# Pooled values by way of a buffer in DRAM, transfers on GpSimd's queue, and another order, in a kernel of pooled attention and mixture of depths

## The chip, the cores and the metric

One core of a Trainium2 chip runs the whole program. Its engines work side by side, each through a queue of its own: PE (matmuls, with the weight load PEld), DVE (vector), ACT (activations), POOL (GpSimd) and SP, which here only issues transfers. All transfers, whoever issues them, run on the core's 16 DMA engines. PSUM, which PE writes, has eight banks; SBUF holds the tiles. The metric is the device time of one execution in microseconds.

## What is computed

The reference, cut. q, k and v are float32 of (8 batches, 8 heads, 576 tokens, 64); the weights are 512 x 1024 and 1024 x 512; capacity is 128.

```python
k_p = k.reshape(B, H, Sp, 8, D).mean(axis=3)        # Sp = 72 pooled keys and values
v_p = v.reshape(B, H, Sp, 8, D).mean(axis=3)
attn = softmax(q @ k_p^T / sqrt(D));  x = attn @ v_p # then (B, S, H*D)
scores = x @ w_gate
for b in range(B):
    top = indices of the 128 highest scores[b]
    ye = relu(x[b, top] @ w1) @ w2
    out[b] = x[b];  out[b, top] += sigmoid(scores[b, top]) * ye
```

## The kernel before

The work is written as some 770 steps. Each step has an engine (or a choice of two), what it reads and writes, and a name. A class Plan can order them by costs; here it is given three tables instead: ORDER is the sequence in which the steps are emitted, and so the order in each engine's queue; HOMES says which PSUM banks each PE job gets; TURNS says which engine of its choices a step takes. Engines wait for one another by semaphores that follow from the tiles read and written.

Per batch there is a **front** and a **dense** part. The front:
- loads the keys (KR, one buffer), the queries (QR, two) and the values (VR, two); a partition of KR and QR holds 36 consecutive tokens of a head, 16 partitions a head;
- pools keys (L498, L499: sums of fours), transposes them in blocks of 32 on DVE (kh, L507), adds the two halves (kt, L512) and sets the eight left-over pooled keys apart (kl, L517);
- transposes the queries on DVE (qt, L526), makes scores on PE (L544, L553) and their exponentials on ACT (em, el);
- pools the values (pool_v): they are loaded with a pooled row of eight tokens in one partition, 64 partitions for each parity of the heads, in eight transfers a batch, and added in three steps, 4 + 4, 2 + 2, 1 + 1 (L571, L575, L576). The sums go to VS, with a column of eights and, after a product with the gate weights (L580, L584), a column of gate scores; VL spreads the left-over rows (L588);
- attends in five chunks of tokens on PE (L605, L609), divides (L632, L633) and stores the rows of x to the output (five transfers);
- ranks: score rows are spread over partitions by PE (L670), copied (sr, L393 or L395), compared on DVE (cmp, L682), made one-hot (oh, L688), and PE **picks** (L694) the chosen tokens' numbers and scores, five columns in one PSUM bank, which DVE reads in two instructions, tk (L698) and gv (L711); POOL makes indices (ix, L702) and gathers 128 rows of x back from the output (xr, L703).

The dense part transposes the gathered rows (L724), multiplies by w1 in eight groups (L733) with relu (ht), by w2 in eight groups (L747), adds (y, L752) and scatters the rows to the output (L756). PE also runs sixteen groups of matmuls on the identity (L775) that nobody reads.

PSUM is three tiles for Plan: pG with four banks, pA and pJ with two each. Transfers of SP and ACT take turns on eight semaphores, so that a transfer waits for the one eight before it. ACT's queue holds transfers between its activations, and SP's holds only transfers; both run strictly in order.

Of the kernel before, what the change touches and what calls it, by code (L numbers as in the profile page):

```python
# [16 lines left out]
def kernel(  # L17
# [58 lines left out]
"""  # L76
HOMES = """
# [3 lines left out]
"""  # L81
TURNS = """
# [165 lines left out]
def direct_path(ctx, tc, q, k, v, moe_w_gate, moe_w1, moe_w2, moe_capacity, out, flag):  # L248
# [46 lines left out]

    KR = sb("kr", [128, TG, D])
    QR = [[sb(f"qr{i}{h}", [128, hi - lo, D]) for h, (lo, hi) in enumerate(HALF)] for i in range(2)]
    VR = sb("vr", [128, NP + 1, POOLW * D], n=2)
    KS = sb("ks", [128, R, D])
    KH = sb("kh", [128, 2, 2 * G, R])  # L300
    KT = sb("kt", [128, 2, 2, SP], n=2)
# [263 lines left out]
    def pool_v(b):  # L565
# [13 lines left out]
        def gate(e):  # L579
            engine(e).tensor_tensor(out=x[:, :, 2], in0=VS[i][:, :, 0:D], in1=WG, op=OP.mult)  # L580
# [603 lines left out]
```

## Time and profile before

| | us |
|---|---|
| runs: median of 2 (lowest, highest) | 309.18 (308.87, 309.48) |
| the profiled execution | 306.87 |
| its span in the trace | 305.0 |
| PE, DVE, POOL, ACT busy in the span | 239.0, 163.6, 126.6, 48.1 |

The rows quoted below come from the profiled execution. Its granted clock of TensorE was 0.908 of full speed on average. A busy PE is one with a matmul under way, whose ends the profile models. "Idle before" names what ended an engine's waiting, as the semaphores let it be inferred.

### The profile page before, as it was taken

How to read it: one execution, taken by the hardware profiler on the slowest of the kernel's cores; microseconds unless marked ns; L12 is line 12 of the kernel's file. 1: busy time of each engine (PE TensorE's matmuls, PEld its weight loads, DVE VectorE, ACT ScalarE, POOL GpSimd, SP SyncE). 2: the span in 40 equal slices, each digit the busy share in tenths (PEclk: the TensorE clock that was granted, in tenths of full speed). 3: DMA queues.
4: the chain of work that ended last, by engine and by line, in shares of the span. 5: the costliest groups of instructions: out<-in, count | busy, mean ns of one | idle time of the engine just before them, and what ended most of it. 6: DMA issues, size and time to landing. Idle time of an engine off the chain costs nothing. (4 is left out here: it accounts for less than half of the span.)

```text
span 305.0 us, 7299 instructions
## 1 busy us (share of the span) xinstructions
PE 239.0 (78%) x3090; PEld 165.3 (54%) x3090; DVE 163.6 (54%) x361; ACT 48.1 (16%) x134; POOL 126.6 (42%) x158
## 2 busy tenths in 40 slices
PE   7395769487597959899859997988667568999980
PEld 7263547156484534688626456768337345688530
DVE  3459592693789746597589697645144320200320
ACT  0021204031214312213210121420002100000000
POOL 3435941665677295789388453100110203100111
PEclk9867979779999986999977999999975969999996
DMA  7989939799977899688863602205120012000001
GB/s 257 201 263 163 376 91 243 222 348 227 368 255 234 198 334 290 164 269 209 269 228 118 177 24 73 90 13 167 49 78 25 0 34 71 0 34 2 34 35 45
DMA packets 18361, 47.87 MB, mean 157 GB/s; under 512 B 2320, under 2 KB 2320, under 8 KB 17424
## 3 DMA queue, kind: packets, MB, share of 16 engines
q1 hardware_dynamic: 9992, 25.37, 28.7%
q10 hardware_dynamic: 7048, 17.76, 20.2%
q0 software_dynamic: 1280, 4.20, 4.2%
q8 instruction: 26, 0.43, 0.6%
q14 instruction: 15, 0.12, 0.2%
HBM read 35.78 MB, written 11.53 MB: 155 GB/s over the span
## 5 line engine op out<-in xcount | busy, mean ns | idle before, releaser
L682 DVE SCALAR_TENSOR_TENSOR cmp<-sr,sc,lat 128x576 bf16<-128x576 f32 (+1 forms) x40 | 39.8, 995 | 10.5 <-ACT sr L393 9.7
L544 PE MATMUL pG<-qt,kt 32*64 32x320 f32 (+1 forms) x512 | 22.8, 468 | 14.7 <-DVE qt L526 5.3
L733 PEld LDWEIGHTS pJ<-xg,w 128*128 128x128 f32 x224 | 26.9, 193 | 5.5 <-issue 3.4
L733 PE MATMUL pJ<-xg,w 128*128 128x128 f32 x224 | 28.4, 278 | 1.6 <-DVE tk L698 1.6
L756 POOL DMA_INDIRECT out_dram<-y,ix x8 | 8.2, 1022 | 47.7 <-DVE y L752 41.7
L747 PE MATMUL pA<-w,ht 128*128 128x512 f32 x48 | 26.8, 677 | 1.0 <-ACT ht L740 1.0
L526 DVE STREAM_TRANSPOSE qt<-qr 128x1280 f32<-128x1280 f32 (+1 forms) x16 | 21.7, 1364 | 9.7 <-DMA qr<-in_q_dram 9.7
L702 POOL TENSOR_SCALAR ix<-tk 128x1 int32<-128x1 f32 x8 | 3.0, 370 | 55.9 <-DVE aux L656 22.6
L747 PE MATMUL pJ<-w,ht 128*128 128x512 f32 x48 | 23.4, 607 | 2.0 <-ACT ht L740 2.0
L544 PEld LDWEIGHTS pG<-qt,kt 32*64 32x64 f32 x512 | 10.3, 142 | 23.2 <-POOL kt L512 6.2
L733 PEld LDWEIGHTS pA<-xg,w 128*128 128x128 f32 x160 | 19.8, 195 | 5.2 <-issue 3.6
L498 POOL TENSOR_TENSOR kr<-kr 128x640 f32<-128x640 f32 (+1 forms) x14 | 20.4, 1458 | 5.1 <-DMA kr<-in_k_dram 5.0
L733 PE MATMUL pA<-xg,w 128*128 128x128 f32 x160 | 20.9, 280 | 1.1 <-ACT xg L393 0.7
L558 ACT ACTIVATE em<-pG 128x1280 f32<-128x1280 f32 (+1 forms) x16 | 18.1, 1128 | 22.4 <-PE pG L553 12.1
L571 POOL TENSOR_TENSOR vr<-vr 128x1280 f32<-128x1280 f32 x6 | 17.4, 2894 | 8.4 <-DMA vr<-in_v_dram 8.1
L733 PEld LDWEIGHTS pG<-xg,w 128*128 128x128 f32 x128 | 18.4, 224 | 3.9 <-issue 1.9
L733 PE MATMUL pG<-xg,w 128*128 128x128 f32 x128 | 19.3, 311 | 0.8 <-ACT xg L393 0.7
L747 PE MATMUL pG<-w,ht 128*128 128x512 f32 x32 | 16.9, 649 | 0.9 <-ACT ht L740 0.7
L688 DVE TENSOR_SCALAR oh<-slots,rk 128x128 bf16<-128x128 f32 x40 | 16.3, 469 | 0.0
L575 POOL TENSOR_TENSOR vr<-vr 128x640 f32<-128x640 f32 x8 | 12.4, 1547 | 8.3 <-DVE every L487 5.2
L605 PE MATMUL pG<-vs,em 64*64 64x66 f32 x480 | 11.9, 222 | 4.8 <-DVE xs L633 2.3
L633 DVE TENSOR_TENSOR xs<-pG,rz 128x512 f32<-128x512 f32 (+1 forms) x17 | 11.7, 690 | 6.5 <-PE pG L609 4.8
(152 smaller groups left out, 390.8 us busy)
## 6 DMA issues: line engine op xcount, KB each, us to landing
kr<-in_k_dram SPq DMA_DIRECT2D x4, 1152.0 KB
out_dram<-xs SPq DMA_DIRECT2D x17, 256.0 KB
out_dram<-xs ACTq DMA_DIRECT2D x15, 256.0 KB
kr<-in_k_dram ACTq DMA_DIRECT2D x3, 1152.0 KB
vr<-in_v_dram SPq DMA_DIRECT2D x9, 384.0 KB
w<-in_moe_w_dram SPq DMA_DIRECT2D x3, 1024.0 KB
vr<-in_v_dram ACTq DMA_DIRECT2D x7, 384.0 KB
qr<-in_q_dram ACTq DMA_DIRECT2D x4, 640.0 KB
```

The costliest lines, as they stand in the source:

```text
L498: e.tensor_tensor(out=x[:, a:z, 0:2], in0=x[:, a:z, 0:2], in1=x[:, a:z, 2:4], op=OP.add)
L526: nc.vector.transpose(out=QT[b % 2][h].rearrange("p j t c -> p t j c"), in_=QR[b % 2][h].rearrange("p t (j e) -> p t j e", j=2))
L544: nc.tensor.matmul(pG[64 * s : 64 * s + 64, r, 0:n], KT[i][rows, j, s, 0:NK], tokens(j, s, rows, 0, hi - lo), start=(j == 0), stop=(j == 1))
L558: nc.scalar.activation(EM[h][i], pG[:, :, 0:n], AF.Exp, scale=exp_scale)
L571: engine(e).tensor_tensor(out=x[:, :, 0:4], in0=x[:, :, 0:4], in1=x[:, :, 4:8], op=OP.add)
L575: engine(e).tensor_tensor(out=x[:, :, 0:2], in0=x[:, :, 0:2], in1=x[:, :, 2:4], op=OP.add)
L605: nc.tensor.matmul(acc[64 * z : 64 * z + 64, s, E * m : E * m + E], EM[h][i][64 * s : 64 * s + 64, m, m0 + 64 * z : m0 + 64 * z + 64], VS[ ...
L633: nc.vector.tensor_tensor(out=XS[i][c][rows].rearrange("p (m s d) -> p s m d", s=2, d=D), in0=o[:, :, :, 0:D], in1=rz.rearrange("p (s m on ...
L682: nc.vector.scalar_tensor_tensor(cmp[0:n], SR[0:n], SC[i][0:n, c : c + 1], LAT[0:n, LAST - OFF[c] : LAST - OFF[c] + S], op0=OP.subtract, o ...
L688: nc.vector.tensor_scalar(OH[:, c, :], slots, RK[:, b, c], None, op0=OP.is_equal)
L733: nc.tensor.matmul(single(ju)[:, cap * f : cap * f + cap], w1[g][:, d, 128 * f : 128 * f + 128], XG[i][:, d, :], start=(d == 0), stop=(d = ...
L747: nc.tensor.matmul(single(jd)[0:cap, :], HT[i][f // 4][:, f % 4, :], w2[f // 4][:, f % 4, :], start=(f == 0), stop=(f == FB - 1))
```

## The change

The values are loaded like the keys, 36 consecutive tokens of a head in a partition, in one transfer a batch. Two steps add them to sums of four tokens (VH, nine half sums a partition), which a transfer stores to a buffer in DRAM, half_sums. Six transfers read them back in the order of the pooled keys, the two half sums of one pooled value beside each other (V2, two buffers), and a third step (L589 in the changed kernel) adds these to VS. The product with the gate weights gets a tile of its own (VM). Transfers may also be issued by POOL; the new TURNS puts thirteen there: the keys of batches 1, 2 and 4, the values of 5, seven stores (six of x, one of half sums) and two read-backs. ORDER and HOMES are new throughout. Up to the first lines of the tables the diff is whole:

```diff
--- before.py
+++ after.py
@@ -46,54 +46,54 @@
 ORDER = """
-    9 2 4 767 3 5 761 760 23 10 757 768 754 22 25 24 26 12 18 17 19 16 20 34 21 11 8 6 27 28 35 36 766 14 39 13 40
...
+    2 4 774 16 0 6 770 772 762 3 5 768 765 14 10 18 9 17 766 11 776 19 20 22 21 763 771 32 33 23 24 767 761 87 34
...
@@ -295,7 +295,10 @@
 
     KR = sb("kr", [128, TG, D])
     QR = [[sb(f"qr{i}{h}", [128, hi - lo, D]) for h, (lo, hi) in enumerate(HALF)] for i in range(2)]
-    VR = sb("vr", [128, NP + 1, POOLW * D], n=2)
+    VR = sb("vr", [128, TG, D], n=2)
+    VH = sb("vh", [128, R, D])
+    V2 = sb("v2", [128, NP + 1, 2, D], n=2)
+    VM = sb("vm", [128, NP + 1, D])
     KS = sb("ks", [128, R, D])
     KH = sb("kh", [128, 2, 2 * G, R])
     KT = sb("kt", [128, 2, 2, SP], n=2)
@@ -363,6 +366,7 @@
         return pG[:, x] if x < 4 else (pA, pJ)[x // 2 - 2][:, x % 2]
 
     out_rows = out.rearrange("b s d -> (b s) d")
+    halves = nc.dram_tensor("half_sums", [B, H, 2 * SP, D], FT, kind="Internal").ap()
     store, scat, gath = {}, {}, {}
 
     def others(ins, b, kinds):
@@ -382,7 +386,7 @@
                 then(i)
         other = ("SP", "ACT")[eng == "SP"]
         return add(eng, cost, go, reads, writes, prio, nbytes=nbytes, rate=rate, name=name, mark=mark,
-                   alts=((eng, cost), (other, cost)))
+                   alts=((eng, cost), (other, cost), ("POOL", 1.05)))
 
     def both(alts, first, fn, *a, **k):
         alts = alts if first else alts[::-1]
@@ -464,18 +468,23 @@
             dma(QR[b % 2][h], src[:, a:z], 128 * 256 * (z - a), p + 2 + 0.1 * h, (), [("QR", b % 2, h)], name=f"q{b}{h}")
 
     def load_v(b):
-        p = 100 * b + 3
+        dma(VR[b % 2], v[b].rearrange("h (g t) d -> (h g) t d", g=G), 128 * 256 * TG, 100 * b + 3, (), [("VR", b % 2)],
+            rate=400e3, name=f"v{b}")
+
+    def place_v(b):
+        i, p = b % 2, 100 * b - 40
+        dma(halves[b].rearrange("h (g r) d -> (h g) r d", g=G), VH, 128 * R * 256, p, ["VH"], [("VD", b)], rate=390e3,
+            name=f"vs{b}")
+        src = halves[b].rearrange("(m s) (n two) d -> s n m (two d)", s=2, two=2)
         for s in range(2):
-            src = v[b].rearrange("(m s) (n t) d -> s n m (t d)", s=2, t=POOLW)[s]
-            for w, (a, z) in enumerate(((0, 48), (48, NK))):
-                dma(VR[b % 2][64 * s + a : 64 * s + z, 0:NP], src[a:z], (z - a) * NP * 2048, p + 0.1 * s, [("VR", b % 2)],
-                    [("VRq", b % 2, s, w)], rate=390e3, name=f"v{b}{s}{'xy'[w]}", cost=0.65)
+            dma(V2[i][64 * s : 64 * s + 64, 0:NP].rearrange("p m two d -> p m (two d)"), src[s, 0:NK], 64 * NP * 512, p + 0.1,
+                [("VD", b), ("V2", i)], [("V2q", i, s, 2)], rate=260e3, name=f"v{b}{s}", cost=0.6)
             for u in range(2):
                 x = 64 * s + 32 * u
-                dma(VR[b % 2][x : x + 32, NP], src[NK:], 32 * 2048, p + 0.3 + 0.1 * s, [("VR", b % 2)],
-                    [("VRq", b % 2, s, 2 + u)], rate=200e3, name=f"v{b}{s}{u}", cost=0.65)
-
-    VQ = [(s, w) for s in range(2) for w in range(4)]
+                dma(V2[i][x : x + 32, NP].rearrange("p two d -> p (two d)"), src[s, NK:], 32 * 512, p + 0.2,
+                    [("VD", b), ("V2", i)], [("V2q", i, s, u)], rate=130e3, name=f"v{b}{s}{u}", cost=0.6)
+
+    VQ = [(s, w) for s in range(2) for w in range(3)]
 
     def load_gate():
         t, o = moe_w_gate.tensor, moe_w_gate.offset
@@ -564,25 +573,29 @@
 
     def pool_v(b):
         i = b % 2
-        x = VR[i].rearrange("p m (w d) -> p m w d", d=D)
+        x = VR[i].rearrange("p (r t) d -> p r t d", t=4)
         p = 100 * b - 40
 
         def one(e):
-            engine(e).tensor_tensor(out=x[:, :, 0:4], in0=x[:, :, 0:4], in1=x[:, :, 4:8], op=OP.add)
-        both((("DVE", 1.52), ("POOL", 3.06)), b < 1, one, [("VRq", i, *a) for a in VQ], [("VR", i)], p, name=f"va{b}")
+            engine(e).tensor_tensor(out=x[:, :, 0:2], in0=x[:, :, 0:2], in1=x[:, :, 2:4], op=OP.add)
+        both((("DVE", 1.4), ("POOL", 2.75)), b < 1, one, [], [("VR", i)], p, name=f"va{b}")
 
         def two(e):
-            engine(e).tensor_tensor(out=x[:, :, 0:2], in0=x[:, :, 0:2], in1=x[:, :, 2:4], op=OP.add)
-            engine(e).tensor_tensor(out=VS[i][:, :, 0:D], in0=x[:, :, 0], in1=x[:, :, 1], op=OP.add)
-        both((("DVE", 1.36), ("POOL", 2.8)), b < 1, two, [], [("VR", i), ("VS", i)], p, name=f"vb{b}")
+            engine(e).tensor_tensor(out=VH, in0=x[:, :, 0], in1=x[:, :, 1], op=OP.add)
+        both((("DVE", 0.8), ("POOL", 1.45)), b < 1, two, [("VR", i)], ["VH"], p, name=f"vb{b}")
+        place_v(b)
+
+        def three(e):
+            engine(e).tensor_tensor(out=VS[i][:, :, 0:D], in0=V2[i][:, :, 0], in1=V2[i][:, :, 1], op=OP.add)
+        both((("DVE", 0.48), ("POOL", 0.95)), b < 1, three, [("V2q", i, *a) for a in VQ], [("V2", i), ("VS", i)], p, name=f"vc{b}")
 
         def gate(e):
-            engine(e).tensor_tensor(out=x[:, :, 2], in0=VS[i][:, :, 0:D], in1=WG, op=OP.mult)
-        both((("DVE", 0.5), ("POOL", 0.88)), False, gate, [("VS", i), ("WG", 0), ("WG", 1), "WGL"], [("VR", i)], p, name=f"vg{b}")
+            engine(e).tensor_tensor(out=VM, in0=VS[i][:, :, 0:D], in1=WG, op=OP.mult)
+        both((("DVE", 0.5), ("POOL", 0.88)), b < 1, gate, [("VS", i), ("WG", 0), ("WG", 1), "WGL"], ["VM"], p, name=f"vg{b}")
 
         def total():
-            nc.vector.tensor_reduce(out=VS[i][:, :, D + 1], in_=x[:, :, 2], axis=AX.X, op=OP.add)
-        add("DVE", 0.48, total, [("VS", i)], [("VR", i), ("VS2", i)], p, name=f"vt{b}")
+            nc.vector.tensor_reduce(out=VS[i][:, :, D + 1], in_=VM, axis=AX.X, op=OP.add)
+        add("DVE", 0.48, total, ["VM", ("VS", i)], [("VS2", i)], p, name=f"vt{b}")
 
         def spread(e):
             engine(e).tensor_tensor(
```

Lines below L300 of the changed kernel stand 4 to 13 lines further down than before: L733 is L746 there, L747 is L760, L694 is L707.

SP's queue from the program's start; vr_72 and vr_73 are the two buffers of raw values, v_75 and v_76 those of the read-back half sums, wg the gate weights. Before:

```order
L380 DMA kr<-in_k_dram 128x1280
L380 DMA vr_72<-in_v_dram 32x1x512
L380 DMA kr<-in_k_dram 128x1024
L380 DMA vr_72<-in_v_dram 32x1x512 x2
L380 DMA vr_72<-in_v_dram 16x4x512
L380 DMA qr_68<-in_q_dram 128x1024
L380 DMA wg<-in_moe_w_gate_dram 64x4x64
L380 DMA vr_73<-in_v_dram 32x1x512 x4
L380 DMA vr_72<-in_v_dram 48x4x512
```

Now:

```order
L384 DMA vr_72<-in_v_dram 128x2304
L384 DMA qr_68<-in_q_dram 128x1024
L384 DMA half_sums<-vh 128x576
L384 DMA wg<-in_moe_w_gate_dram 64x4x64
L384 DMA v_75<-half_sums 64x4x128
L384 DMA v_75<-half_sums 32x1x128 x3
L384 DMA qr_71<-in_q_dram 128x1280
L384 DMA v_76<-half_sums 64x4x128 x2
L384 DMA v_76<-half_sums 32x1x128
L384 DMA half_sums<-vh 128x576
```

The eight pieces of a batch's values are one row now, and the store of half sums and the read-back that waits for it stand ahead of the queries of batch 1 (qr_71).

DVE's queue at the first front; kr and ks are keys, qt transposed queries, vs pooled values, vm the product with the gate weights. Before:

```order
L507 STREAM_TRANSPOSE kh<-ks 128x9x64
L526 STREAM_TRANSPOSE qt_81<-qr_69 128x20x2x32
L571 TENSOR_TENSOR vr_72<-vr_72 128x5x256
L487 TENSOR_TENSOR every<-inside 128x4
L488 TENSOR_SCALAR wg<-wg,every 128x64
L490 SCALAR_TENSOR_TENSOR wg<-wg,every 128x64 x3
L401 MEMSET eps 128x1
L526 STREAM_TRANSPOSE qt_80<-qr_68 128x16x2x32
L443 TENSOR_SCALAR lat<-lat 128x1088
L580 TENSOR_TENSOR vr_72<-vs_92,wg 128x5x64
L584 TENSOR_REDUCE vs_92<-vr_72 128x5
```

Now:

```order
L535 STREAM_TRANSPOSE qt_84<-qr_68 128x16x2x32
L526 TENSOR_TENSOR kl_82<-kt_80,inrow 128x128
L447 TENSOR_SCALAR lat<-lat 128x1088
L535 STREAM_TRANSPOSE qt_85<-qr_69 128x20x2x32
L496 TENSOR_TENSOR every<-inside 128x4
L497 TENSOR_SCALAR wg<-wg,every 128x64
L499 SCALAR_TENSOR_TENSOR wg<-wg,every 128x64 x3
L507 TENSOR_TENSOR kr<-kr 128x4x128
L508 TENSOR_TENSOR ks<-kr 128x256
L589 TENSOR_TENSOR vs_96<-v_75 128x5x64
L593 TENSOR_TENSOR vm<-vs_96,wg 128x320
L597 TENSOR_REDUCE vs_96<-vm 128x5
```

The first add of the values has left DVE; both query transposes stand ahead of the gate weights' row, and the third add (L589) stands behind the keys of batch 1.

PE's queue from the last of batch 5's five picks to the next transposes of gathered rows (the trace counts two instructions for each matmul in float32 here). Before:

```order
L694 MATMUL pG<-aux_115,oh 128x5
L733 MATMUL pA<-xg_137,w_145 128x128 x8
L670 MATMUL pG<-ident,sc_111 128x128 x2
L733 MATMUL pA<-xg_137,w_145 128x128 x8
L670 MATMUL pG<-ident,sc_112 128x128 x2
L733 MATMUL pA<-xg_137,w_146 128x128 x8
L670 MATMUL pJ<-ident,sc_112 128x128 x3
L747 MATMUL pG<-w_147,ht_141 128x512 x4
L724 MATMUL pG<-ident,xr_134 128x128 x4
```

Now, from the same pick to the transposes:

```order
L707 MATMUL pA<-aux_119,oh 128x5
L746 MATMUL pJ<-xg_142,w_150 128x128 x4
L746 MATMUL pG<-xg_141,w_149 128x128 x4
L683 MATMUL pA<-ident,sc_115 128x128 x2
L683 MATMUL pG<-ident,sc_116 128x128 x2
L760 MATMUL pJ<-w_152,ht_146 128x512
L683 MATMUL pA<-ident,sc_116 128x128 x3
L760 MATMUL pJ<-w_152,ht_146 128x512
L746 MATMUL pJ<-xg_141,w_150 128x128 x8
L737 MATMUL pG<-ident,xr_138 128x128 x4
```

The pick has moved from pG to pA, and the groups that follow it write to pJ and pG; before, the scores' spreads and the second products that follow it write to pG.

## Rows read from the trace of the kernel before

**Rows 1.** Page, parts 1 to 3: busy times, DMA share in 40 slices, packets.

```profile
PE 239.0 (78%) x3090; PEld 165.3 (54%) x3090; DVE 163.6 (54%) x361; ACT 48.1 (16%) x134; POOL 126.6 (42%) x158
...
DMA  7989939799977899688863602205120012000001
...
DMA packets 18361, 47.87 MB, mean 157 GB/s; under 512 B 2320, under 2 KB 2320, under 8 KB 17424
```

**Rows 2.** Stretches: length, busy time (instructions) by engine, granted clock, DMA share, GB/s.

```profile
0.00:160.00 160.00, 120.42 (x2031) 85.74 (x2032) 106.79 (x207) 33.15 (x97) 96.46 (x122) 0.90 0.86 248
160.00:206.30 46.30, 43.33 (x689) 28.59 (x687) 33.66 (x77) 9.53 (x24) 18.34 (x20) 0.96 0.29 84
206.30:293.50 87.20, 72.62 (x367) 50.12 (x366) 21.40 (x73) 5.37 (x13) 9.90 (x14) 0.90 0.13 42
216.50:248.30 31.80, 19.07 (x81) 12.84 (x81) 11.18 (x38) 3.49 (x9) 4.90 (x6) 0.80 0.14 41
```

**Rows 3.** Timeline of 196 to 306 us: start, length, instruction, idle time before it.

```profile
208.23 0.27 PE L694 MATMUL pG<-aux,oh 128*128 128x5 bf16 x5 [0.82 <-DVE xs L633]
...
216.48 0.16 DVE L698 TENSOR_REDUCE tk<-pG 128x1 f32<-128x2 f32 x1 [3.67 <-PE pG L747]
...
230.34 0.39 PE L694 MATMUL pJ<-aux,oh 128*128 128x5 bf16 x5 [4.42 <-ACT sr L393]
...
241.28 0.16 DVE L698 TENSOR_REDUCE tk<-pJ 128x1 f32<-128x2 f32 x1 [9.21 <-PE pJ L747]
```

**Rows 4.** Chain that ended last: start, length, what it was; unit prices of PE's groups.

```profile
157.81 0.30 PE pG L694 x5
...
248.29 2.08 PE pG L733 x8
...
261.40 0.44 PE pJ L724 x4
...
264.41 0.86 PE pA L747 x2
...
267.06 0.89 PE pG L733 x8
```

**Rows 5.** The same chain: gathers from the output (xr) and a scatter to it.

```profile
217.53 3.39 DMA xr<-out_dram,ix
...
221.72 2.75 DMA out_dram<-y,ix
...
242.59 3.86 DMA xr<-out_dram,ix
```

**Rows 6.** Timeline of 14 to 52 us: first scores, attends and query transposes.

```profile
14.99 2.44 PE L544 MATMUL pG<-qt,kt 32*64 32x320 f32 x32 [5.32 <-DVE qt L526]
...
33.53 0.70 PE L605 MATMUL pJ<-vs,em 64*64 64x66 f32 x32 [1.67 <-POOL vr L571]
...
38.23 1.51 DVE L526 STREAM_TRANSPOSE qt<-qr 128x1280 f32<-128x1280 f32 x1 [3.52 <-DMA qr<-in_q_dram]
...
44.46 1.33 PE L544 MATMUL pG<-qt,kt 32*64 32x320 f32 x32
```

**Rows 7.** Stretches of two loads, columns as in rows 2.

```profile
22.90:30.50 7.60, 3.88 (x54) 2.64 (x55) 7.39 (x10) 1.24 (x1) 4.33 (x4) 0.78 0.98 163
30.50:38.10 7.60, 5.47 (x152) 4.21 (x150) 4.17 (x2) 2.15 (x8) 7.29 (x6) 0.99 0.99 376
```

**Rows 8.** DMA packets of 22.9 to 30.5 us.

```profile
DMA packets 673, 1.24 MB, mean 163 GB/s; under 512 B 77, under 2 KB 77, under 8 KB 670
```

**Rows 9.** Groups by line and shape, POOL: busy us, mean ns, idle time before.

```profile
L571 POOL TENSOR_TENSOR vr<-vr 128x1280 f32<-128x1280 f32 x6 | 17.4, 2894 | 8.4 <-DMA vr<-in_v_dram 8.1 <-issue 0.3
...
L575 POOL TENSOR_TENSOR vr<-vr 128x640 f32<-128x640 f32 x8 | 12.4, 1547 | 8.3 <-DVE every L487 5.2 <-DVE vr L571 2.9
...
L576 POOL TENSOR_TENSOR vs<-vr 128x320 f32<-128x320 f32 x8 | 8.7, 1090 | 0.6
...
L756 POOL DMA_INDIRECT out_dram<-y,ix x8 | 8.2, 1022 | 47.7 <-DVE y L752 41.7 <-DMA xr<-out_dram,ix 3.1 <-DMA out_dram<-y,ix 2.5
```

86 rows, old and new, of tables (HOMES, ORDER, TURNS) are left out of this document.

## The prediction

> **What bounds the kernel now.** I read the page's busy times and slices first: PE is busy 78% of the span, and the DMA row stands mostly at 7 to 9 tenths through the first half of the span and falls to 2 and below after it [rows 1]. The table by stretches says where which of the two is full [rows 2]: up to 160 us DMA is busy 0.86 of the time and PE 120.42 of 160 us; from 160 to 206.3 us, where the last attend ends, PE is busy 43.33 of 46.3 us and DMA 0.29; from there to the last matmul at 293.5 us there is only the dense work, and PE, which has nothing else to do, is busy 72.62 of 87.2 us at a granted clock of 0.90. So there are two limits: the transfers set the pace of the fronts (pool, scores, attend of a batch) in the first half, and PE with its own waits sets the tail. Engines that are idle elsewhere (POOL 42%, ACT 16% of the span) set nothing by their totals.
>
> Next I read the tail as a timeline. PE's picks of batch 5 (L694) start at 208.23 us and last 0.27 us, yet DVE reads the result (tk, L698) only at 216.48 us, and its last 3.67 us of idle time were ended by matmuls of L747 into pG, another job's work in the same tile [rows 3]. The gather (from 217.53 us, [rows 5]), PE's transposes and the products behind them follow from that. Batch 6 does the same again: picks at 230.34, read at 241.28 us after 9.21 us of idle time that a product into pJ ended. The two readings are 8.0 (216.48 minus 208.50) and 10.5 us (241.28 minus 230.73) later than their input. In 216.5 to 248.3 us PE is therefore busy 19.07 of 31.8 us, at a clock of 0.80 [rows 2].
>
> What the tail must cost: after the last attend there stand 72 groups of dense work, in both kernels (before: 32 of L733 and 40 of L747; now 36 and 36). A group of L733 takes 0.89 us and one of L747 0.86 us at full clock, against 2.08 for a group of L733 at a low one [rows 4]. 36 times 0.89 and 36 times 0.86 make 63.0 us; four batches' transposes at 0.44 and three batches' picks at 0.30 are 2.7 us more. So 65.7 of the 87.2 us are work, and 21.5 us are lost.
>
> **The change, part by part.** *The order in the tail.* In the new order the picks of batch 5 go to pA and those of 6 and 7 to pJ, and what PE writes next goes to other tiles, so that DVE's reading is not tied to a later matmul; PE has 6 or 7 groups between a pick and the transposes that need its gather. From tk to the gather's start there is 1.05 us (216.48 to 217.53), and the gather takes 3.39 to 3.86 us [rows 3, 5]; with 0.3 us of picks that is some 5 us, and 6 groups at 0.86 to 0.89 cover it. I credit 12 us: the idle time of 216.5 to 248.3 us is 12.7. The rest of the 21.5 us (the low clock and half-microsecond waits for relu) I leave, since new waits of that kind can stand in the new order. Bounds: 0 if other readings are tied in the same way, 21.5 if none is.
>
> *The start.* The first scores run at 14.99 us, the first attend at 33.53, the second batch's first scores only at 44.46 us [rows 6]: DVE waits for its queries until 38.23 us before it transposes them, and PE first does the last attend of batch 0. In the new order those queries are issued early, the keys of batch 1 come through POOL's queue as soon as DVE has freed the tile, and DVE has the pooled values of batch 0 right behind the keys. The new first step is not free: the values of batch 0 are read whole (1.18 MB) beside the keys, pooled on POOL in 2.6 and 1.5 us (see below), stored, read back and added. I put the first attend at 28 to 31 us and the second batch's scores at 37 us: a gain of 7. It holds as far as fronts, not transfers, are late; bounds 0 and 12.
>
> *The bytes.* By the shapes, the values were 5120 pieces of 2 KB (10.49 MB); they become 1024 of 9216 B (9.44 MB), plus the half sums, stored in 1024 pieces of 2304 B (2.36 MB) and read back in 5120 pieces of 512 B (2.62 MB): 3.93 MB more in all, on 47.87 MB [rows 1]. At the mean of the first 160 us, 248 GB/s, this is 15.8 us, if transfers bound every one of them. Against it, the stretch 22.9 to 30.5 us moved nearly only 2 KB pieces of values: DMA share 0.98, 163 GB/s, 670 of 673 packets under 8 KB [rows 7, 8]. The stretch after it, with keys in 9216 B pieces and queries in 4 to 5 KB ones, has the same share, 0.99, at 376 GB/s. By these two the old load is 10.49 MB at 163, 64.4 us of busy DMA; the new one 9.44 MB at 376, 25.1, and the 4.98 MB of half sums at 163, 30.6: a gain of 8.7 us. No row shows 512 B pieces, and I take them to be slower per byte than 2 KB ones, so I stand nearer the loss: plus 4, bounds minus 9 and plus 16.
>
> [...]
>
> *POOL and DVE.* Per batch the adds on POOL took 2.89, 1.55 and 1.09 us [rows 9]. The new ones have 1152, 576 and 320 elements per partition; between the rows of 640 and 1280 and those of 320 and 640 this is 2.6, 1.5 and 1.1: 0.3 us less, 3 over eight batches. POOL gets 13 transfers to issue; by its indirect ones at 1.02 us [rows 9] that is 13 to 14 us more. Cover: POOL is busy 96.46 of the first 160 us [rows 2] and would be at 107. But it runs in order: behind a transfer that waits stand the key adds and the score rows (kt, kl), for which PE waits. I charge 0, and 6 if half of the issue time falls on a chain. DVE gives away the first adds of batches 0 and 7 and gets three third adds, a quarter as long each, and batch 0's spread: 0.
>
> *New waits.* The store of half sums waits for POOL's or DVE's second add, and the read-back for the store's landing; on SP the loads behind them wait too (the next queries, the next values). Nearest rows: a scatter to DRAM 2.75 us, a gather from it 3.39 [rows 5], 6.1 us for the round trip on an almost idle DMA. The order has the first adds one to two batches ahead of the attends, which hides it; uncovered it is 6.1 us a batch.
>
> *Sum.* The profiled execution took 306.87 us (span 305.0); 306.87 - 12 - 7 + 4 = 291.9. The runs' median, 309.18, is 2.3 above the profiled one, so the forecast is **294 us**. No difference under 2%, some 6 us, counts as a change here.
>
> **Rivals.** *More of the tail comes back.* If no reading is tied and the clock stays up, 21.5 in place of 12, and the bytes cost nothing: 306.87 - 21.5 - 7 + 2.3 = 281 us. For: the work itself leaves PE without gaps in the new order. Against: ties by tile between relu, copies and products remain, and the clock was low where PE had just stood waiting for a gather.
>
> *The bytes take the gain.* With plus 16 for the transfers and no gain at the start the time is 306.87 - 12 + 16 + 2.3 = 313; with the bytes as forecast and the tail's 12 lost to other ties, 306. For: DMA is busy 0.86 up to 160 us. Against: 160 to 206.3 us has 0.29, so inputs that come some us later need not move the last attend. This is also how the change would fail to do what it says: larger pieces that move no faster.
>
> *The round trip takes the fronts' slack: slower.* Place: SP's queue, where a store waits for an add, the read-back for the store, and the next batch's loads stand behind both; and POOL's third add, which waits for six landings. Price: 6.1 us a front. With the start's gain gone, 306.87 - 12 + 4 + 2.3 = 301.2; the second uncovered front (313) is slower than before, the third (319.5) by more than 2%. For: the first front has the whole trip on its path. Against: from the second on, the values are pooled one to two batches ahead.
>
> **How the numbers follow.** Forecast (288 to 302) 0.44; more of the tail 0.20; bytes or new ties 0.22; round trip 0.14. The first two are below 303.0, 2% under the median: faster 0.64. The third lies between 303 and 315.4: same 0.22. Slower 0.14. For the range I leave out the lower half of the 281 us case, and the round trip from the third front on: **280 to 318 us**.
>
> **What would show it.** Tail: from the last attend to the last matmul some 75 us, tk within a microsecond of its picks, clock near 1 all through. Start: first attend at about 30 us, the second batch's scores before 40. Bytes: some 51.8 MB, and stretches of value loads near 376 GB/s. Round trip: POOL's third add (L589) not waiting for half sums after the first batch. I am wrong if the last attend ends after 206 us, which the DMA row up to there would explain, or if tk again waits for products.

## The result, and the profile after

The changed kernel takes 286.08 us (median of 2 runs, 285.76 to 286.40) against 309.18: the ratio is 0.925, 95% interval 0.919 to 0.931. The forecast was 294, range 280 to 318. The profiled execution took 285.76 us (span 284.0), 21.1 us less than that of before. Executions that took over 1.5% longer than the fastest of their kernel are in the medians and ranges below, but not in the ratios, and the profiles of a_tie and a_wide are of such executions.

The page of the changed kernel, parts 1 to 3, as in [rows 1]:

```profile
PE 229.4 (81%) x3090; PEld 160.8 (57%) x3090; DVE 162.6 (57%) x365; ACT 46.6 (16%) x132; POOL 130.4 (46%) x169
...
DMA packets 20446, 51.82 MB, mean 182 GB/s; under 512 B 2820, under 2 KB 7876, under 8 KB 18484
```

PE runs the same 3090 matmul instructions, and DVE, ACT and POOL are busy within 4 us of before; the bytes rise by 3.95 MB (3.93 forecast). The table by stretches, up to the end of the last attend (200.1 us) and of the last product (273.8 us), columns as in [rows 2]:

```profile
0.00:160.00 160.00, 123.90 (x2002) 88.63 (x2002) 108.51 (x216) 31.10 (x86) 96.36 (x119) 0.88 0.81 273
160.00:200.10 40.10, 37.25 (x686) 23.14 (x686) 30.81 (x83) 9.79 (x30) 18.20 (x25) 1.00 0.33 101
200.10:273.80 73.70, 68.15 (x404) 49.05 (x403) 22.32 (x64) 5.74 (x16) 14.88 (x25) 1.00 0.16 50
```

DMA is less busy up to 160 us (0.81 for 0.86) although it moves more bytes. The last attend ends 6.2 us earlier. For the tail one thing has to be put right first: [rows 2] ended it at 293.5 us, but the timeline of before has products until 293.24 + 2.74 = 296.0:

```profile
293.24 2.74 PE L747 MATMUL pJ<-w,ht 128*128 128x512 f32 x6
```

So the tail was 89.7 us and is 73.7 now, 16.0 less; of the 89.7, by the prediction's price of the work (65.7), 24.0 were lost and not 21.5. From there to the end of the span it is 9.0 us before and 10.2 after. 6.2 and 16.0 less 1.2 are the 21.0 us by which the span is shorter.

The timeline of the tail after; the rows answer to [rows 3] (L707 are the picks, L711 is tk):

```profile
203.58 0.27 PE L707 MATMUL pA<-aux,oh 128*128 128x5 bf16 x5
...
203.97 0.15 DVE L711 TENSOR_REDUCE tk<-pA 128x1 f32<-128x2 f32 x1
...
221.36 0.27 PE L707 MATMUL pJ<-aux,oh 128*128 128x5 bf16 x5
...
222.54 0.15 DVE L711 TENSOR_REDUCE tk<-pJ 128x1 f32<-128x2 f32 x1
225.93 1.09 POOL L716 DMA_INDIRECT xr<-out_dram,ix  x1 [2.37 <-DMA out_dram<-xs]
...
229.38 0.66 PE L737 MATMUL pG<-ident,xr 128*128 128x128 f32 x4 [0.71 <-DMA xr<-out_dram,ix]
...
232.48 0.27 PE L707 MATMUL pJ<-aux,oh 128*128 128x5 bf16 x5
232.79 0.16 DVE L711 TENSOR_REDUCE tk<-pJ 128x1 f32<-128x2 f32 x1 [0.24 <-PE pJ L707]
```

tk begins 0.4, 1.2 and 0.3 us after the start of its picks. The second gather now waits for a store of x instead.

The timeline of the start, as in [rows 6] (L553 scores of the second batch, L618 attends, L589 the third add of the values):

```profile
25.92 0.49 DVE L589 TENSOR_TENSOR vs<-v 128x320 f32<-128x320 f32 x1 [3.45 <-DMA v<-half_sums]
...
29.81 1.16 PE L618 MATMUL pA<-vs,em 64*64 64x66 f32 x32 [6.23 <-DVE vs L597]
...
38.38 1.34 PE L553 MATMUL pG<-qt,kt 32*64 32x320 f32 x32 [0.28 <-DVE rz L645]
```

The first attend begins at 29.8 us and the second batch's scores at 38.4, as forecast. But the half sums are waited for, and not in the first batch alone. Who waited for the buffer, by the view of one tile (us, times; ACT's 18.6 us run from the start of the span to its first activation, which stands behind two of the read-backs in its queue):

```profile
  ACT L571: 18.6, 1
  POOL vs L589: 12.6, 4
  ACT em L567: 6.2, 1
  DVE vs L589: 3.4, 1
...
```

SP's own queue stood longest behind the stores of half sums, by its table of waits (sum, times, longest):

```profile
SPq L384 <- DMA half_sums<-vh: 57.7, 7, 20.1
```

### The profile page after: what moved, and what is told of

It reads as the page before. It is cut to its first block, busy times and chain, and to the rows that moved or that the text cites. A ratio compares the mean times of both kernels' runs of the same rounds, so it can differ in the third digit from the quotient of the medians.

```text
span 284.0 us, 7279 instructions
## 1 busy us (share of the span) xinstructions
PE 229.4 (81%) x3090; PEld 160.8 (57%) x3090; DVE 162.6 (57%) x365; ACT 46.6 (16%) x132; POOL 130.4 (46%) x169
## 3 DMA queue, kind: packets, MB, share of 16 engines
q10 hardware_dynamic: 6836, 17.60, 18.6%
## 4 chain that ended last, share of the span: by engine, by line
PE 53%; DMA 22%; DVE 12%; issue 3%; POOL 3%; ACT 2%; SPq 1%; ACTq 0%; POOLq 0%; DVEq 0%
PE pJ L760 8%; DMA xr<-out_dram,ix 7%; PE pG L760 7%; PE pJ L746 7%; DMA half_sums<-vh 5%; PE pG L746 5%; PE pG L553 5%; DMA vr<-in_v_dram 5%; PE pA L746 3%; PE pG L618 3%; DMA v<-half_sums 3%; DVE cmp L695 3%; DMA out_dram<-xs 3%; PE pG L562 3%; PE pG L622 3%
## 5 line engine op out<-in xcount | busy, mean ns | idle before, releaser
L760 PE MATMUL pJ<-w,ht 128*128 128x512 f32 x64 | 32.2, 624 | 3.2 <-DVE tk L711 2.3
L746 PE MATMUL pJ<-xg,w 128*128 128x128 f32 x256 | 32.1, 281 | 3.1 <-ACT ht L753 2.3
L746 PEld LDWEIGHTS pJ<-xg,w 128*128 128x128 f32 x256 | 30.7, 195 | 6.7 <-ACT ht L753 2.7
L553 PE MATMUL pG<-qt,kt 32*64 32x256 f32 (+1 forms) x512 | 22.6, 466 | 9.0 <-ACT el L571 5.7
L580 POOL TENSOR_TENSOR vr<-vr 128x1152 f32<-128x1152 f32 x8 | 22.2, 2775 | 5.6 <-DMA vr<-in_v_dram 5.6
L535 DVE STREAM_TRANSPOSE qt<-qr 128x1024 f32<-128x1024 f32 (+1 forms) x16 | 21.7, 1363 | 2.8 <-DMA qr<-in_q_dram 2.8
L760 PE MATMUL pG<-w,ht 128*128 128x512 f32 x48 | 22.3, 594 | 0.0
L567 ACT ACTIVATE em<-pG 128x1024 f32<-128x1024 f32 (+1 forms) x16 | 18.1, 1129 | 25.5 <-PE pG L562 19.3
L746 PEld LDWEIGHTS pG<-xg,w 128*128 128x128 f32 x160 | 19.0, 192 | 4.3 <-issue 1.9
L746 PE MATMUL pG<-xg,w 128*128 128x128 f32 x160 | 19.7, 276 | 1.4 <-DVE y L765 0.8
L618 PEld LDWEIGHTS pG<-vs,em 64*64 64x64 f32 x560 | 13.4, 151 | 13.0 <-issue 5.8
L553 PEld LDWEIGHTS pG<-qt,kt 32*64 32x64 f32 x512 | 10.5, 146 | 16.5 <-issue 10.2
L618 PE MATMUL pG<-vs,em 64*64 64x66 f32 x560 | 14.6, 241 | 6.1 <-DVE xs L646 2.3
L618 PEld LDWEIGHTS pA<-vs,em 64*64 64x64 f32 x480 | 12.1, 146 | 11.1 <-DVE vs L597 6.6
L760 PEld LDWEIGHTS pJ<-w,ht 128*128 128x128 f32 x64 | 11.0, 193 | 12.8 <-issue 8.1
L618 PE MATMUL pA<-vs,em 64*64 64x66 f32 x480 | 13.0, 233 | 6.2 <-DVE vs L597 6.2
L622 PE MATMUL pG<-vl,el 64*64 64x264 f32 x140 | 13.9, 445 | 1.3 <-POOL vl L601 1.3
```

The source lines that it names most:

```text
L535: nc.vector.transpose(out=QT[b % 2][h].rearrange("p j t c -> p t j c"), in_=QR[b % 2][h].rearrange("p t (j e) -> p t j e", j=2))
L553: nc.tensor.matmul(pG[64 * s : 64 * s + 64, r, 0:n], KT[i][rows, j, s, 0:NK], tokens(j, s, rows, 0, hi - lo), start=(j == 0), stop=(j == 1))
L567: nc.scalar.activation(EM[h][i], pG[:, :, 0:n], AF.Exp, scale=exp_scale)
L580: engine(e).tensor_tensor(out=x[:, :, 0:2], in0=x[:, :, 0:2], in1=x[:, :, 2:4], op=OP.add)
L618: nc.tensor.matmul(acc[64 * z : 64 * z + 64, s, E * m : E * m + E], EM[h][i][64 * s : 64 * s + 64, m, m0 + 64 * z : m0 + 64 * z + 64], VS[ ...
L622: nc.tensor.matmul(acc[64 * z : 64 * z + 64, s, 0 : NP * E], EL[h][i][64 * s : 64 * s + 64, l0 + 64 * z : l0 + 64 * z + 64], VL[i][64 * s ...
```

## The experiments

Times are medians of 4 runs (before and after: 2; b_64: 10), each beside runs of the kernel before on the same chip, whose median was 307.8 to 309.9; the ratio is to these, with half an interval of 0.005 to 0.018. Differences in microseconds below are between medians; taken by the ratios they shift by up to 3 us. The last two columns are read from each profile's timeline: the end of the last attend, and from there to the end of the last product.

| run | us (lowest to highest) | ratio to before | last attend | tail |
|---|---|---|---|---|
| before | 309.18 | | 206.3 | 89.7 |
| after | 286.08 (285.76 to 286.40) | 0.925 | 200.1 | 73.7 |
| b_untied | 290.56 (286.58 to 292.47) | 0.940 | 208.7 | 70.5 |
| a_tie | 296.45 (294.52 to 299.53) | 0.966 | 201.8 | 85.3 |
| b_bigv | 284.47 (283.62 to 286.62) | 0.929 | 183.1 | 89.8 |
| b_2kwide | 285.80 (283.22 to 288.98) | 0.919 | 186.1 | 89.2 |
| b_64 | 304.27 (301.83 to 308.29) | 0.991 | 201.4 | 89.6 |
| a_oldv | 302.52 (301.32 to 304.44) | 0.984 | 219.3 | 73.9 |
| a_notrip | 278.98 (277.88 to 280.09) | 0.908 | 194.5 | 73.6 |
| a_double | 307.50 (302.23 to 309.81) | none given | 220.1 | 73.9 |
| a_nopool | 291.10 (288.44 to 292.89) | 0.936 | 203.1 | 78.1 |
| f_new | 317.60 (316.24 to 318.70) | 1.027 | 235.1 | 70.5 |
| a_wide | 281.61 (277.71 to 286.57) | 0.910 | 197.0 | 73.7 |
| g_wide | 267.40 (265.93 to 268.75) | 0.869 | 187.2 | 70.5 |

The two columns move apart: the way of the values changes the first and hardly the second, the ties the second and hardly the first (a_nopool moves both a little). That is the frame for what follows.

**Theories.** T: the tail is long because readings stand behind products into the same tile. Rival: PE's order and banks themselves count. For the fronts, V: the new way of the values costs bytes, and the order brings the gain (the forecast). Rival: the old load was slow, and the new load is the gain.

**b_untied: the ties taken out of the kernel before.** tk of the last three batches (with gv of batch 6) and one copy are emitted earlier. For the copy no queue changes, only the write that it waits for; in DVE's queue the readings move, here at batches 6 and 7 (batch 5 likewise):

```
 L688 TENSOR_SCALAR oh<-slots,rk 128x128 x5
-L682 SCALAR_TENSOR_TENSOR cmp,rk<-sr,sc_112,lat 128x576 x2
 L698 TENSOR_REDUCE tk_123<-pJ 128x1
 L711 TENSOR_REDUCE gv_131<-pJ 128x1
-L682 SCALAR_TENSOR_TENSOR cmp,rk<-sr,sc_112,lat 128x576 x2
+L682 SCALAR_TENSOR_TENSOR cmp,rk<-sr,sc_112,lat 128x576 x4
 L682 SCALAR_TENSOR_TENSOR cmp,rk<-sr,sc_112,lat 64x576
 L688 TENSOR_SCALAR oh<-slots,rk 128x128 x5
+L698 TENSOR_REDUCE tk_124<-pJ 128x1
 L752 SCALAR_TENSOR_TENSOR y_144<-pG,gv_132,xr_136 128x512
```

> The kernel before, with the queues of PE, ACT, POOL and SP unchanged: only the readings of the three last picks (tk of batches 5, 6 and 7) and the copy of batch 6's score row (L393) are emitted ahead of the products that write to the same PSUM tile behind them; on DVE those readings move up by a few instructions. Theory of the ties (a reading emitted behind a product into the same tile waits for that product, and this is what the tail before loses): tk of batch 5 about 0.3 us behind its picks instead of 8.0, the compares of batch 6 begin near 214 us instead of 225.2, PE idle in the tail down by 8 to 12 us, and with a better clock the time is 296 to 301 us. Rival (the order of PE's queue is what counts): PE, whose queue is unchanged, waits next for the gather and for relu, and the time stays within 3 us of 309.

Measured: 290.56 us, ratio 0.926 to 0.955. The copy of batch 6's score row (L393) in the kernel before, then the timeline of b_untied (L694 picks, L682 compares of batch 6) and its tail by stretches:

```profile
224.88 0.32 ACT L393 COPY sr<-pG 128x192 f32<-128x192 f32 x1 [19.99 <-PE pG L747]
```

```profile
210.57 0.27 PE L694 MATMUL pG<-aux,oh 128*128 128x5 bf16 x5 [0.82 <-DVE xs L633]
212.99 0.16 DVE L698 TENSOR_REDUCE tk<-pG 128x1 f32<-128x2 f32 x1 [0.23 <-PE pG L670]
...
215.25 0.32 ACT L393 COPY sr<-pG 128x192 f32<-128x192 f32 x1 [8.01 <-DVE aux L656]
...
215.96 0.81 DVE L682 SCALAR_TENSOR_TENSOR cmp<-sr,sc,lat 128x576 bf16<-128x576 f32 x1
...
223.50 0.27 PE L694 MATMUL pJ<-aux,oh 128*128 128x5 bf16 x5
```

```profile
208.20:279.20 71.00, 67.62 (x382) 46.25 (x372) 22.21 (x74) 5.25 (x13) 11.34 (x15) 1.00 0.16 53
```

The compares of batch 6 begin at 215.96 and its picks at 223.50 (230.34 in [rows 3]). With PE's queue unchanged the tail is 19.2 us shorter and the clock in it 1.00 instead of 0.90. T holds, and the time is below the expected 296 to 301 us. The copy, which the forecast had not listed, was tied as well: it comes 9.6 us earlier. tk of batch 5 comes 2.4 us behind its picks, not 0.3; by the row it still waits for a score row's spreads (L670) into pG. The run took the four ties out together and does not price them one by one.

**a_tie: two ties put back into the changed kernel.** In the table of banks batch 6's picks go to bank 0 (pG) and batch 7's to the other bank of pJ; tk of batch 7 stands behind two L746 groups (in DVE's queue it changes places with gv).

> The changed kernel with two ties put back, every engine's queue as it is but for gv and tk of batch 7 changing places: batch 6's picks get a bank of pG, so that tk stands behind the product L760 into pG that follows two L746 groups later, and batch 7's tk is emitted behind the two L746 groups into pJ that follow its picks. Theory of the ties: tk of batch 6 at about 228.7 us instead of 222.5 and its gather 3 to 4 us later (there it waits for a store of x until 225 us now), tk of batch 7 another 3.5 us behind its picks, PE waits before the transposes of both batches, 290 to 294 us. Rival (PE's order in the changed kernel has groups enough to cover late readings): 288 us or less.

Measured: 296.45 us, 10 more than the changed kernel. The timeline:

```profile
230.62 0.16 DVE L711 TENSOR_REDUCE tk<-pG 128x1 f32<-128x2 f32 x1 [1.62 <-PE pG L760]
...
235.75 1.09 PE L737 MATMUL pG<-ident,xr 128*128 128x128 f32 x4 [5.17 <-DMA xr<-out_dram,ix]
...
241.21 0.27 PE L707 MATMUL pJ<-aux,oh 128*128 128x5 bf16 x5
...
245.12 0.16 DVE L711 TENSOR_REDUCE tk<-pJ 128x1 f32<-128x2 f32 x1 [3.45 <-PE pJ L746]
```

PE waits 5.17 us for a gather for which it waited 0.71 in the changed kernel. The tail is 11.6 us longer, and the time beyond the range I gave: the late gather puts batch 6's transposes 6.4 us later than in the changed kernel, batch 7's picks 8.7 (241.21 for 232.48), and batch 7's transposes, with the second tie, 11.7 (249.65 for 238.00).

**b_bigv, b_2kwide, b_64: the load alone, in the kernel before.** The eight transfers of a batch become one of 36 tokens a partition (b_bigv); or two that keep the 2 KB pieces, the main one over 128 partitions (b_2kwide); or two of 64 partitions for the main rows, with the four of the left-over rows as before (b_64). Lines of the three diffs, cut:

```
-dma(VR[b % 2][64 * s + a : 64 * s + z, 0:NP], src[a:z], ...)          # eight a batch, 16 to 48 partitions
+dma_start(out=VR[b % 2].rearrange("p m x -> p (m x)")[:, 0 : TG * D], in_=big)                   # b_bigv
+dma_start(out=VR[b % 2][:, 0:NP], in_=rows[0:512].rearrange("(m p) x -> p m x", p=128))          # b_2kwide
+dma_start(out=VR[b % 2][64 * o : 64 * o + 64, 0:NP], in_=both_[o, 0:NK])   # b_64, o = 0 and 1
```

> The kernel before, with one load of 36 consecutive tokens a partition in place of the eight transfers of a batch's values, at the place of the first of them; the adds stay as they are, so the values are added in the wrong grouping and the last 256 columns are zero: this leaves out the right pooling, and there is no round trip and no half sums. If the transfers set the pace of the fronts up to 160 us (64.4 us of busy DMA become 25.1), the last attend comes at 196 us or earlier instead of 206.3 and the time is 300 us or less. If the fronts' pace is set by the chain through DVE, POOL and PE, the DMA share falls but the last attend stays within 3 us and the time within 306 to 312 us.

> The kernel before with the values still read in pieces of 2 KB, but in two transfers a batch, the first of them over all 128 partitions, instead of eight over 16 to 48; pooled rows come to other partitions, so the right order of the pooled values is left out; no round trip, no half sums. If the size of the pieces made the old load slow, the stretches of value loads stay near 163 GB/s and the time near 309 us. If it was their narrow spread over partitions, they run at 300 GB/s or more and the time falls to that of the load in one transfer, 284 to 290 us.

> The kernel before, with the main rows of the values read in two transfers of 64 partitions each (0 to 63, then 64 to 127), one behind the other on one queue, in pieces of 2 KB; the left-over rows as before, outputs right. [...] If it was the cutting into eight small transfers that was slow: 284 to 290 us, like the load over 128 partitions.

Measured: 284.47, 285.80 and 304.27 us. One load in the old order brings the last attend forward by 23.2 us, more than the whole change does, and pieces of 2 KB to 128 partitions do about as well as pieces of 9 KB (20.2 us for 23.2). To 64 partitions they gain 4.9 us (0.9% by the ratio). A stretch of b_64 in which 2 KB pieces go to 64 partitions, and one of g_wide (below) in which they go to 128, columns as in [rows 2]:

```profile
20.00:24.00 4.00, 3.02 (x61) 2.27 (x60) 3.97 (x6) 0.00 (x0) 2.28 (x2) 1.00 1.04 184
```

```profile
9.00:12.00 3.00, 1.20 (x11) 1.01 (x10) 2.85 (x4) 0.75 (x1) 1.90 (x7) 1.00 0.99 376
```

With nearly the same busy share and the same pieces it is 184 against 376 GB/s, and 163 for the eight transfers of before [rows 7]. The transfers of b_64 are also smaller, 512 KB for 1 MB. But the loss is in each packet and not between transfers: the busy time of the queue that carries these pieces, over its packets, makes 0.17 us a packet in the stretches of before and of b_64, and 0.09 us in that of g_wide.

**a_oldv: the old load in the changed kernel's order.**

> The changed kernel's order, homes and tail, with the values loaded as before (eight transfers a batch in pieces of 2 KB, four on SP and four on ACT where the changed kernel has its one load; pooled in place in three adds, no half sums, no round trip). The forecast's account (the new value path costs 4 us, the order brings the rest): 280 to 284 us, faster than the 286.1 of the changed kernel. Rival (larger pieces free the DMA engines, worth 9 us or more in the fronts): 292 to 300 us, with DMA near 1 and 163 GB/s in the stretches of value loads and the last attend back near 206 us.

Measured: 302.52 us, 16.4 more than the changed kernel; the last attend is 19.2 us later, the tail the same. That is above even the rival's range of 292 to 300. V falls: the new way of the values, trip and all, is worth 16 us in this order. The size has a reservation: at the start the eight pieces stand near the head of both queues, and already the first attend comes at 39.3 us.

**a_notrip and a_double: what the half sums cost.** a_notrip reads the input in their place; a_double makes each store and read-back twice.

```
-        src = halves[b].rearrange("(m s) (n two) d -> s n m (two d)", s=2, two=2)
+        src = v[b][:, 0 : 2 * SP].rearrange("(m s) (n two) d -> s n m (two d)", s=2, two=2)      # a_notrip
+            if twin:                                                                             # a_double
+                engine(e).dma_start(out=twin[0], in_=twin[1])
```

> The changed kernel, with the read-back taken from the values in the input (same shapes, same pieces of 512 B) instead of the half sums, so that it doesn't wait for the second add and the store; the store is still made, and nobody reads it. This leaves out the right pooled values. Forecast (the round trip is hidden but for the first batch): 282 to 286 us, first attend 2 to 6 us earlier, no more than 4 us in all. Rival (an uncovered round trip of some 6 us in each front): 270 us or less.

> The changed kernel with the traffic of the half sums doubled: each store is made a second time to a buffer that nobody reads, each read-back a second time to a tile that nobody reads, right behind the first on the same queue (4.98 MB and eight transfers a batch more). If the bytes of the half sums bind (the forecast's bounds: 512 B pieces no faster than the 163 GB/s of the old values), 30 us of busy DMA are added and the time is 296 us or more. If these pieces are cheap and what the half sums cost is the waiting for them, the time is 286 to 291 us.

Measured: 278.98 and 307.50 us. The wait for the trip costs 7.1 us (5.5 by the ratios) with all its bytes still moved, between the two expectations. Doubled traffic costs 16 to 24 us (its runs spread from 302.23 to 309.81), so it is not cheap; but the run doubles transfers, their places in the queues of SP and ACT and the time until they land together, and which of these counts it does not tell. Pieces of 512 B were not seen to be slower per byte than the old load with its 163 GB/s. Packets of the changed kernel from 30 to 34 us, 565 of them (under 2 KB, not under 512 B) read-backs:

```profile
DMA packets 849, 0.99 MB, mean 247 GB/s; under 512 B 77, under 2 KB 642, under 8 KB 841
```

The read-backs are only 0.29 of these 0.99 MB. In a purer stretch, 18.5 to 19.5 us, with 334 of 367 packets of that kind, it is 234 GB/s at a busy share of 1.00.

**a_nopool: POOL's 13 transfers on SP** (thirteen numbers of TURNS from 2 to 0).

> The changed kernel with the 13 transfers of POOL's queue moved to SP's queue at the same places of the order. Forecast (issuing on POOL costs nothing): 284 to 289 us. Rival 1 (POOL's issue time lies on a chain): 280 us or less. Rival 2 (SP's queue, which waits for the half sums, holds up the keys of batches 1, 2 and 4 and the values of 5 behind it): 290 us or more, second batch's scores later than 38.4 us.

Measured: 291.10 us, 5.0 more, or 3.2 by the ratios, whose intervals overlap (0.927 to 0.945 here, 0.919 to 0.931 for the changed kernel): inconclusive. Rival 1 is out; rival 2 has the time at most and not its mark, since the second batch's scores stay at 38.4 us. In its profile the last attend is 3.0 us later and the tail 4.4 us longer.

**f_new: the round trip in the old order.**

> A third order: the new path of the values (one load, half sums stored and read back on SP's queue, right outputs) put into the order and homes of the kernel before, with the three readings of picks and the score copy emitted early as in the run that untied them; no transfer on POOL; the second add stands right behind the first, and the third add in batches 1, 2, 4 and 7 right ahead of the column of gate scores. If the gains of larger pieces (24 us) and of the untied tail (18 us) are independent and the round trip costs up to 12 us here: 267 to 280 us. If they are one gain counted twice: 284 us or more.

Measured: 317.60 us, slower than before (1.019 to 1.035). The tail is the short one, 70.5 us; the last attend comes at 235.1. POOL's table of waits (sum, times, longest):

```profile
POOL vs L589 <- DMA v<-half_sums: 63.6, 8, 9.7
```

8.0 us a front, in all eight: the slower rival of the forecast, in an order that puts the second add too near the third. The time is over 284 us, but not for the reason expected: the tail's gain came in full, and the trip took far more than the 12 us allowed for it.

**a_wide and g_wide: a wide load without half sums.** If the main pooled keys of an even head are its rows 8 to 71, the 128 rows of a pair of heads lie at one stride, and one transfer loads them (lines of the diff, cut):

```
+    MAIN, LEFT = (SP - NK, 0), (0, NK)
+        wide = v[b].rearrange("h (n t) d -> (h n) (t d)", t=POOLW).rearrange("(m r) x -> r m x", r=2 * SP)[SP - NK : SP - NK + 128]
+                        engine(e).dma_start(out=VR[b % 2][:, 0:NP], in_=wide)
-                        nc.tensor.matmul(pG[...], KT[i][rows, j, s, 0:NK],
+                        nc.tensor.matmul(pG[...], KT[i][rows, j, s, MAIN[s] : MAIN[s] + NK],
```

a_wide has it in the changed kernel's order, g_wide in that of b_untied.

> The changed kernel's order, homes and tail, without half sums: the main rows of the values in one transfer over 128 partitions at the place of its one load, the left-over rows in four transfers of 32 partitions behind it on SP and ACT, three adds in place, outputs right. If the new order is worth nothing of its own in the fronts and only the round trip held it back: 272 to 280 us (the run without the round trip's wait took 279.0). If the new order's fronts are slower than those of the old order once both have a wide load: 283 us or more.

> A version that computes the right outputs without half sums: the kernel before, untied as in the earlier run, with the 64 main pooled rows of the values read in one transfer over all 128 partitions (pieces of 2 KB), for which the main pooled keys of an even head become rows 8 to 71 and its left-over ones rows 0 to 7; the four transfers of the left-over rows stay. If the untied tail (18 us) and the wide load (24 us) are independent: 264 to 272 us, faster than the changed kernel's 286. If they are one gain counted twice: 280 us or more.

Measured: 281.61 and 267.40 us. g_wide is the fastest kernel here, 0.869 of before (0.859 to 0.880), 18.7 us under the changed one: the two gains add up. a_wide lies between its two expectations, and its interval, 0.891 to 0.928, reaches into both; it is above that of g_wide all the same. The stretches of g_wide:

```profile
0.00:160.00 160.00, 133.72 (x2137) 95.12 (x2138) 123.36 (x234) 35.82 (x102) 109.82 (x139) 0.94 0.76 263
...
186.80:257.80 71.00, 67.62 (x380) 46.25 (x372) 22.22 (x74) 5.26 (x13) 11.62 (x15) 1.00 0.16 53
```

With a wide load in both, the new order ends its fronts 9.8 us later than the old one and has a tail 3.2 us longer.

## Why the prediction was right, and where its steps were not

*The tail, minus 12:* right in mechanism, 16.0 measured. Two parts were undersized. PE's idle time fell from 14.6 us (89.8 less 75.22 busy, to 296.1 us) to 5.6 (73.7 less 68.15), 9.0 us; and I left the low clock in, but with most of the gaps gone it rose from 0.90 to 1.00, and PE was busy 7.1 us less for the same 72 groups. b_untied and a_tie show the cause from both sides. The order of PE's queue was not needed for it.

*The start, minus 7:* the marks came (first attend 29.8, second batch's scores 38.4), the cause did not. I gave it to the order. b_bigv, in the old order, has 26.8 and 36.3 us, and a_oldv, in the new one, 39.3 and 48.4: the start follows the load of the values. It does so at half the rate too (184 GB/s in b_64, 376 in g_wide): b_64 has 26.1 and 38.1 us. So at the start the eight pieces or their places in the queues cost more than the rate does; no run tells these two apart.

*The bytes, plus 4:* **this step failed.** I set the 163 GB/s of the old load against the 376 of the next stretch [rows 7], put the difference down to the size of the pieces, and took pieces of 512 B to be worse still, for which I had no row; the stretch of nearly only such pieces moved 234 GB/s. By b_2kwide and b_64 the size was not it: with pieces of 2 KB throughout, the rate went with the number of partitions that a transfer writes, 163 GB/s with the old transfers to 16 to 48 each, 184 to 64 (b_64), 376 to 128 (g_wide). In place of plus 4 the new way of the values is worth minus 16 in the new order (a_oldv), and the load by itself minus 23 in the old one (b_bigv).

*New waits, 0 after the first batch:* wrong. The third add waited for half sums in the first batch and in four others (16.0 us in all by the rows above), and the wait is worth 7.1 us (a_notrip). The price for a front, 6.1 us, came out at 8.0 in f_new, where nothing hides it.

*POOL, 0:* not refuted. a_nopool, 3 to 5 us slower with overlapping intervals, leaves room for a small gain by POOL's queue, which I had bounded only as a cost.

*The sum.* For the fronts I had minus 3 (minus 7, plus 4), and 6.2 came; for the tail 12, and 16.0 came. The fronts' small number hides large ones. From the last attends, step by step: minus 19.1 for the wide load with the ties out (206.3 to 187.2, g_wide), plus 9.8 for the new order with the same load (197.0, a_wide), plus 3.1 for the half sums in place of that load (200.1). With the old load the new order costs 13.0 (219.3, a_oldv). So the fronts had two terms of the wrong sign, the order as a gain of 7 and the new way of the values as a loss of 4, and it was luck that their errors nearly cancelled; the tail's term was right for its reason. Why the new order's fronts are slower by themselves is not settled: no run took that apart.

## What to carry to other kernels

Before blaming the size of a transfer's pieces, look at how many partitions it writes: two loads with pieces of the same size (b_64 and b_2kwide, 304.27 and 285.80 us here) cost one run each and would have turned the sign of my term. Where waits are kept by tile, a reading belongs right behind the write that it needs, ahead of any other write into that tile; that can be had by emitting it earlier, without touching the busy engine's queue (b_untied: a tail of 70.5 us for 89.7). A round trip through DRAM had a price for each front that showed in full in the order that did not hide it (8.0 us in f_new), so a layout that needs none is worth a search first.

## What the hardware showed that I had not expected

Pieces of 2 KB came into SBUF at 163 GB/s in transfers to 16 to 48 partitions, at 184 to 64, and at 376 to 128, each with the DMA engines 0.98 to 1.04 busy: the engines look equally full, and only GB/s beside the share tells them apart. The slower two took 0.17 us a packet where the fastest took 0.09; why fewer partitions go with a longer time for each packet no run here shows.

Beside other traffic a short trip was long: the first batch's half sums were added by 10.2 us (the second add on POOL began at 8.81 and took 1.40), their read-back was issued from 16.48 on, and they were used at 25.92, 15.7 us after the add, where a scatter and a gather on an almost idle DMA took 6.1 [rows 5].
